# A linear-attention block with a gated convolution: the convolution moved to VectorE, g moved into x, the first loads split between two queues, and a new written-out order

## The chip, the cores and the metric

The kernel runs on one core of a Trainium2 chip. The metric is the device time of one execution in microseconds (us); less is better. The core's engines work from queues of their own, each strictly in its own order, and wait for each other on semaphores: TensorE (PE, matmuls into PSUM; its weight loads are shown apart as PEld), VectorE (DVE), ScalarE (ACT), GpSimd (POOL, which here only issues transfers) and SyncE (SP, which only issues transfers too).

## The reference

There are 8 batches (b), 8 heads, 576 rows (s), a head width of 64, a model width of 512 and a hidden width of 1024.

```
kv   = k^T v                          per batch and head, 64 x 64
o    = q kv
x    = o / sqrt(mean(o*o) + 1e-6) * g     (mean over the 64 of a head; heads side by side: 512)
h    = relu(x @ w_in)                 576 x 1024
c    = cw[0]*h[s-1] + cw[1]*h[s] + cw[2]*h[s+1]     per channel, zero outside
out  = (h * sigmoid(c)) @ w_out       576 x 512, fp32
```

All inputs and the output are fp32 in DRAM.

## The kernel before, in words

Everything on the chip is transposed: channels lie on the 128 partitions and the 576 rows of a batch along the free axis. The 512 model channels are 4 tiles t of two heads each; the 1024 hidden channels are 8 blocks f. The program is a list of small steps, written out by hand in the string ORDER (lines 62 to 105). A token such as `hm.3.4` calls the function `hm` with batch 3 and block 4, which issues its few instructions. The order of the tokens is the order of every engine's queue; the loop at line 540 ties each instruction to the one before it on its engine, so nothing is moved by a scheduler. The steps are:

- `Lq`, `Lk`, `Lv` (line 148): POOL loads q, k or v of a batch, cast from fp32 to bf16 on the way, into one of two buffers each. A buffer is free again when `qt` or `kv` of the batch that used it is done, and POOL waits for that with all that stands behind it.
- `kv` (272): k^T v on TensorE, 48 small matmuls; `kvc` (284, 286) copies it to a block-diagonal bf16 tile, on ScalarE, for batch 0 half on VectorE.
- `qt` (296): q transposed on TensorE, two tiles t in one step; `qc` (303) copies it to SBUF on VectorE. The rows stand in a permuted order (six interleaved groups of 96), which a later step undoes by a strided read (`natural`).
- `ot` (308, 309): o = q kv. `sq` (328) squares it and `oc` (334) copies it out, both on ScalarE.
- The norm: batch 0 by `on` (sums by a matmul with ones), `nl` (348, reciprocal square root on ScalarE) and `mu0` (357, x on VectorE). The others by `ss` (373), `ln` (383, with a table load before it and another before the next sigmoid), `sl` (391 to 394, the factor split in three bf16 parts), `sp` (403, spread back over the partitions by a matmul) and `mu` (409, x = o times the factor, on VectorE). Batch 1 has its own `ln`, then pairs 2 and 3, 4 and 5, 6 and 7.
- `ws` (261): g is multiplied into w_in on VectorE, from an fp32 staging tile to bf16. The staging tile comes in three pieces, one by SyncE and two by POOL.
- `hm` (426): one block f of x @ w_in, 8 matmuls of 288 columns; `re` (432): ReLU to bf16 on ScalarE.
- The convolution, in six groups c: batch 0; batch 1; batches 2 and 3; 4 and 5; 6; 7. For batch 0 it is done on TensorE: `di` (480) makes 24 diagonal matrices of cw on VectorE, `cv` (492) is six matmuls per block, `sv` (500) the sigmoid on ScalarE, `mv` (506) the product with h on VectorE. For the other groups: `ta` (451) makes three tap products of a block f on VectorE, `ad` (458, 459) adds them with a shift of one row, two blocks at a time, `sg` (465) takes the sigmoid of both blocks on ScalarE, `mg` (471) multiplies h by it on VectorE.
- `om` (516): 128 rows of the output, 8 matmuls of 512 columns, for a pair of batches p and one of nine row tiles m; `ea` (522) copies it out on ScalarE; `st` (532) stores it, on SyncE's queue.

PSUM is held in two pools: three large buffers ("a", for qt, ot, on, sp, hm, cv) and two small ones ("b", for kv, ss, om). Buffers of a pool are handed out in turn.

```python
CONV = {0: (0, 1, 'P'), 1: (1, 1, 'D'), 2: (2, 2, 'D'), 3: (4, 2, 'D'), 4: (6, 1, 'D'), 5: (7, 1, 'D')}
```

Each entry is (first batch, batches, engine).

## Time and profile before

| | |
|---|---|
| time, median of 3 runs | 203.81 us (203.37 to 204.84) |
| profiled execution: its span, first to last instruction | 201.0 us; the page gives no other time for it |
| busy: TensorE, VectorE, ScalarE | 175.3, 155.3, 145.9 us |
| granted TensorE clock | 1.000 |
| DMA: packets, bytes | 26295, 27.03 MB |
| transfers: median time from issue to landing | k, v, q pieces of 576 KB: 11.3, 13.6, 12.6 us; of 144 KB: 9.4 and 9.2 us; SyncE's 512 KB of w_in 3.4 us |
| VectorE: tap products; the two adds; product with h | 43.8; 19.8 + 20.1; 19.8 us |
| TensorE: hm, om (busy, matmuls overlap) | 69.9, 64.1 us |

The profile is one execution. Its page gives busy times, the span in 40 equal slices (each digit the busy tenths of 5 us), the chain of work that ended last, and groups of equal instructions with the mean duration of one. Sizes of transfers are those of the destination: a bf16 piece of 576 KB is 1.18 MB of fp32 in DRAM. A matmul's duration in the groups overlaps with its neighbours; its step from start to start is shorter.

### The profile page before, as it was taken

Reading aid. Unit: us, or ns where it says so; the run is one execution under the profiler, and the core shown is the slowest. Engines: PE = TensorE matmul, PEld = TensorE weight load, DVE = VectorE, ACT = ScalarE, POOL = GpSimd, SP = SyncE. Lnnn points to the kernel's source line nnn. Section 1 sums busy time; section 2 is a strip of 40 time slices with the busy share of each in tenths; the row PEclk is TensorE's granted clock in tenths of the full one; section 3 lists DMA queues with packets and bytes.
Section 4 is the critical chain, followed back from the end, with each engine's and each line's share of the span. In section 5 each row is a group of like instructions: output and inputs, shape, how many; then the busy total and the mean of one; then the engine's idle time right before and its main releaser. Section 6 shows DMA issues by size and latency. Waiting matters only on the chain.

```text
span 201.0 us, 4350 instructions
## 1 busy us (share of the span) xinstructions
PE 175.3 (87%) x1783; PEld 111.8 (56%) x1801; DVE 155.3 (77%) x325; ACT 145.9 (73%) x222; POOL 25.4 (13%) x38
## 2 busy tenths in 40 slices
PE   0057299799998999999999999999999999999792
PEld 0043057477775657766575776445667774444340
DVE  3097921458879799799899999989799999999400
ACT  2006516995999979999678899999978865684532
POOL 7373403103132303100000000000000000000000
PEclk9999999999999999999999999999999999999999
DMA  5999999999999999970200020070005001423654
GB/s 120 146 221 306 198 205 205 204 203 204 204 190 185 201 203 207 202 119 3 104 5 3 0 104 3 7 306 2 3 0 209 3 0 51 159 108 118 247 229 188
DMA packets 26295, 27.03 MB, mean 134 GB/s; under 512 B 1292, under 2 KB 21284, under 8 KB 26276
## 3 DMA queue, kind: packets, MB, share of 16 engines
q0 software_dynamic: 20368, 16.78, 52.4%
q1 hardware_dynamic: 5908, 9.98, 13.1%
q8 instruction: 14, 0.23, 0.4%
q14 instruction: 5, 0.04, 0.1%
HBM read 32.52 MB, written 9.44 MB: 209 GB/s over the span
## 4 chain that ended last, share of the span: by engine, by line
PE 59%; DVE 22%; DMA 10%; ACT 5%; issue 2%; POOL 1%; DVEq 0%; POOLq 0%; ACTq 0%
PE h_ps L426 25%; PE om_ps L516 18%; DVE tap L451 8%; DMA w_stage<-in_moe_w_in_dram 5%; DMA q_sb<-in_q_dram 5%; DVE h L471 4%; PE qt_ps L296 4%; DVE tap L459 3%; PE kv_ps L272 3%; PE sp_ps L403 3%; DVE tap L458 3%; PE cv_ps L492 3%; DVE xT L409 2%; PE o_ps L309 2%; ACT tap L465 2%
## 5 line engine op out<-in xcount | busy, mean ns | idle before, releaser
L426 PE MATMUL h_ps<-xT,w_in_sb 128*128 128x288 bf16 x512 | 69.9, 291 | 3.1 <-DVE w_in_sb L261 2.4
L516 PE MATMUL om_ps<-w_out_sb,h 128*128 128x512 bf16 x278 | 64.1, 379 | 1.5 <-DVE h L471 1.0
L426 PEld LDWEIGHTS <-w_in_sb 128*128 128x128 bf16 x512 | 49.9, 99 | 18.8 <-DVE w_in_sb L261 2.5
L432 ACT ACTIVATE h<-h_ps 128x576 bf16<-128x576 f32 x64 | 41.0, 656 | 14.9 <-PE h_ps L426 14.5
L516 PEld LDWEIGHTS <-h 128*128 128x128 bf16 x288 | 28.0, 98 | 32.2 <-DVE h L471 1.5
L451 DVE TENSOR_SCALAR tap<-h,cw 128x576 bf16<-128x576 bf16 (+1 forms) x120 | 43.8, 428 | 1.8 <-ACT h L432 1.3
L522 ACT ACTIVATE row<-om_ps 128x512 f32<-128x512 f32 x36 | 22.1, 618 | 15.6 <-PE om_ps L516 13.1
L465 ACT ACTIVATE tap<-tap 128x1152 bf16<-128x1152 bf16 (+1 forms) x20 | 31.1, 1553 | 1.6 <-DVE tap L459 1.5
L409 DVE TENSOR_TENSOR xT<-o,sp_ps 128x576 bf16<-128x576 f32 x28 | 20.1, 749 | 5.0 <-PE sp_ps L403 4.8
L471 DVE TENSOR_TENSOR h<-h,tap 128x1152 bf16<-128x1152 bf16 (+1 forms) x20 | 19.8, 992 | 1.8 <-ACT tap L465 1.8
L459 DVE TENSOR_TENSOR tap<-tap 128x1150 bf16<-128x1150 bf16 (+1 forms) x20 | 20.1, 1004 | 0.7
L303 DVE COPY qT<-qt_ps 128x1152 bf16<-128x1152 bf16 x16 | 11.8, 754 | 11.1 <-PE qt_ps L296 10.9
L458 DVE TENSOR_TENSOR tap<-tap 128x1150 bf16<-128x1150 bf16 (+1 forms) x20 | 19.8, 991 | 0.0
L328 ACT ACTIVATE sq<-o_ps 128x576 bf16<-128x576 f32 x28 | 18.2, 689 | 0.5 <-PE o_ps L309 0.5
L334 ACT ACTIVATE o<-o_ps 128x576 f32<-128x576 f32 x28 | 18.1, 677 | 0.5 <-ACT row L522 0.5
L286 ACT ACTIVATE kvbd<-kv_ps 64x256 bf16<-64x256 f32 (+1 forms) x18 | 6.0, 339 | 12.2 <-PE kv_ps L272 11.8
L148 POOL DMA_DIRECT2D k_sb<-in_k_dram x11 | 8.0, 723 | 35.9 <-PE kv_ps L272 35.9
L296 PE MATMUL qt_ps<-ident,q_sb 96*64 96x96 bf16 x384 | 11.2, 217 | 1.4 <-DMA q_sb<-in_q_dram 1.1
L296 PEld LDWEIGHTS <-q_sb 96*64 96x64 bf16 x384 | 9.6, 117 | 3.3 <-issue 2.1
L403 PE MATMUL sp_ps<-wparts,spread 128*128 128x288 bf16 x56 | 9.8, 286 | 0.2 <-DVE xT L409 0.2
L272 PEld LDWEIGHTS <-k_sb 96*64 96x64 bf16 x384 | 8.0, 123 | 3.3 <-issue 3.3
L309 PE MATMUL o_ps<-qT,kvbd 128*128 128x512 bf16 x25 | 9.6, 407 | 0.0
(55 smaller groups left out, 114.9 us busy)
## 6 DMA issues: line engine op xcount, KB each, us to landing
out_dram<-row SPq DMA_DIRECT2D x36, 256.0 KB, 2.3
q_sb<-in_q_dram POOLq DMA_DIRECT2D x8, 576.0 KB, 12.6
k_sb<-in_k_dram POOLq DMA_DIRECT2D x7, 576.0 KB, 11.3
v_sb<-in_v_dram POOLq DMA_DIRECT2D x7, 576.0 KB, 13.6
w_stage<-in_moe_w_in_dram POOLq DMA_DIRECT2D x1, 1024.0 KB, 9.9
w_out_sb<-in_moe_w_out_dram POOLq DMA_DIRECT2D x1, 1024.0 KB, 19.9
...
```

The source lines that it names most:

```text
L296: nc.tensor.transpose(ps[i * D:(i + 1) * D, tt, r * PS:(r + 1) * PS], q_sb[:, 2 * (2 * u + tt) + i, r * D:(r + 1) * D], ident[:PS, :PS])
L328: nc.scalar.activation(s.rearrange("p (n r) -> p n r", r=R), natural(src), AX.Square)
L409: nc.vector.tensor_mul(x_tile(b)[:, t, :].rearrange("p (e n) -> p e n", e=2), T["o32", b, t].rearrange("p (e n) -> p e n", e=2), T["sp", b ...
L426: nc.tensor.matmul(ps[:, e, :HS], w_in_sb[:, t, f * P:(f + 1) * P], x[:, t, e * HS:(e + 1) * HS], start=(t == 0), stop=(t == NT - 1))
L432: nc.scalar.activation(h_tile(b // 2)[:, f, b % 2, :].rearrange("p (e n) -> p e n", e=2), T["hm", b, f][:, :, :HS], AX.Relu)
L451: nc.vector.tensor_scalar_mul(tap[:, m, f % 2, :, :].rearrange("p b s -> p (b s)"), h_tile(p)[:, f, bs, :].rearrange("p b s -> p (b s)"), ...
L458: nc.vector.tensor_add(tap[:, 1, :, 1:], tap[:, 1, :, 1:], tap[:, 0, :, :S - 1])
L459: nc.vector.tensor_add(tap[:, 1, :, :S - 1], tap[:, 1, :, :S - 1], tap[:, 2, :, 1:])
L465: nc.scalar.activation(tap, tap, AX.Sigmoid)
L471: nc.vector.tensor_mul(h, h, T["tap", c, j][:, 1])
L516: nc.tensor.matmul(ps, h[:, f, m * P:(m + 1) * P], w_out_sb[:, f, :], start=(f == 0), stop=(f == NF - 1))
L522: nc.scalar.activation(T["os", p, m], T["om", p, m], AX.Copy)
```

## The change

- The convolution of batch 0 goes to VectorE like the others; `di`, `cv`, `sv`, `mv` and the diagonals are gone.
- The centre tap is no longer a product of its own. cw[0] and cw[2] are divided by cw[1] once (`pc`; cw[1] is kept away from zero), so c = cw[1] * (h + a*h[s-1] + b*h[s+1]), and cw[1] is the scale of the sigmoid's instruction. The scale is per block, so `sg` is one instruction per block f, not per two. `ta` makes two products, `aa` adds them with their shifts, `ab` adds h. The taps lie in two fixed tiles, rows 584 apart.
- g is multiplied into x: `mu` and `mu0` become scalar_tensor_tensor (o * g * factor). `ws` and the staging of w_in are gone; w_in is loaded straight to bf16 by POOL in two halves (`Li`), w_out in two halves (`Lo`).
- Batch 0: the heads of tiles t = 0, 1 come as fp32 by SyncE into the later h buffer and are cast by `ca` (q on ScalarE, k and v on VectorE); those of t = 2, 3 by POOL as before. `qt0` transposes one tile; `qc0` copies it on ScalarE and undoes the permutation there, so `mu0` reads plain rows. All `kvc` of batch 0 are on VectorE.
- Batch 1's loads are in halves of four heads. cw and g are issued from ScalarE's queue.
- `om` of the first and last pair of batches is in two steps of four blocks, with the same matmuls.
- Every buffer is named in the order (`hm.0.1@2`: PSUM buffer a2). The sets of buffers are as large as before. The order is new: among others batch 5's kv stands before batch 4's, and loads follow that.

```diff
-CONV = {0: (0, 1, 'P'), 1: (1, 1, 'D'), 2: (2, 2, 'D'), 3: (4, 2, 'D'), 4: (6, 1, 'D'), 5: (7, 1, 'D')}
+CONV = {0: (0, 1), 1: (1, 1), 2: (2, 2), 3: (4, 2), 4: (6, 1), 5: (7, 1)}
...
+pre@0,0,0,1 ca.q.0 qt0.0@0 qc0.0@0 ca.k.0 ca.v.0 kv.0.0.1@0 kvc.0.0.1.0 kvc.0.0.1.1 ot.0.0@1 sq.0.0@0 on.0@2
+ca.v.1 ca.k.1 ca.q.1 qt0.1@0 kv.0.1.1@1 kvc.0.1.1.1 nl.0@0 Lk.1.0@1 qc0.1 kvc.0.1.1.0 qt0.2@2 ot.0.1@0
+kv.0.2.1@0 qc0.2@1 sq.0.1@1 kv.0.3.1@1 on.1@2 kvc.0.2.1.0 mu0.0@0 kvc.0.2.1.1 nl.1@1 ot.0.2@1 kvc.0.3.1.0
+Lv.1.0@1 sq.0.2@2 ct@0 on.2@2 nl.2@2 kvc.0.3.1.1 mu0.1 Lq.1.0@1 Li.0 pc Lk.1.2 qt0.3@0 mu0.2 qc0.3 ot.0.3@2
+sq.0.3@3 kv.1.0.2@1 on.3@0 kvc.1.0.2.0 pl Lq.1.2 qt.1.0@1 nl.3@3 mu0.3 hm.0.0@0 re.0.0@0 qc.1.0@2 kvc.1.0.2.1
...
+    def ring(r, shape, dtype, name, **kw):
+        s = slots.pop(0)
+        p = psum if r in "ab" else work
+        return p.tile(shape, dtype, name=name, tag=f"{r}{s}", bufs=1, **kw)
...
+    def pre():
...
+        T["stg"] = ring("h", [PS, 3, 2, 2, R * D], FP32, name="stg")
+        for t in range(2):
+            for x in "kvq":
+                nc.sync.dma_start(out=T["stg"][:, "kvq".index(x), t], in_=heads(x, 0, 2 * t, 2))
+        nc.scalar.dma_start(out=cw_rows, in_=moe_conv_w.rearrange("k (f p) -> (k f) p", p=P))
+        for i in range(2):
+            nc.scalar.dma_start(out=g_sb[i * D:(i + 1) * D, :], in_=g_norm.unsqueeze(1))
+        act_table("rs")
...
+        for t in range(2, NT):
+            for x in "kvq":
+                nc.gpsimd.dma_start(out=qkv[x, 0][:, 2 * t:2 * t + 2, :], in_=heads(x, 0, 2 * t, 2))
...
+    def pc():
+        c1 = slice(NF, 2 * NF)
+        tmp = consts.tile([P, 3, NF], FP32, name="ctmp")
+        nc.vector.tensor_copy(cw, T["cw"])
+        nc.vector.tensor_scalar(tmp[:, 0], cw[:, c1], 0.0, 0.5, op0=AL.is_ge, op1=AL.subtract)
+        nc.vector.tensor_mul(tmp[:, 1], cw[:, c1], tmp[:, 0])
+        nc.vector.tensor_scalar(tmp[:, 1], tmp[:, 1], 5e-21, 4.0, op0=AL.max, op1=AL.mult)
+        nc.vector.tensor_mul(cw[:, c1], tmp[:, 0], tmp[:, 1])
+        nc.vector.reciprocal(tmp[:, 2], cw[:, c1])
+        nc.vector.tensor_mul(cw[:, 0:NF], cw[:, 0:NF], tmp[:, 2])
+        nc.vector.tensor_mul(cw[:, 2 * NF:], cw[:, 2 * NF:], tmp[:, 2])
...
+    def ca(x, t):
+        to, fr = qkv[x, 0][:, 2 * t:2 * t + 2, :], T["stg"][:, "kvq".index(x), t]
+        if x == "q":
+            nc.scalar.activation(to, fr, AX.Copy)
+        else:
+            nc.vector.tensor_copy(to, fr)
...
-        if b == 0 and i == 1:
+        if b == 0:
             nc.vector.tensor_copy(to, fr)
         else:
             nc.scalar.activation(to, fr, AX.Copy)
...
+    def qc0(t):
...
+        nc.scalar.activation(by_r(T["qT", 0, t]), natural(T["qt0", t][:, :S]), AX.Copy)
...
-        nc.vector.tensor_mul(
+        nc.vector.scalar_tensor_tensor(
             x_tile(b)[:, t, :].rearrange("p (e n) -> p e n", e=2),
-            T["o32", b, t].rearrange("p (e n) -> p e n", e=2), T["sp", b, t][:, :, :HS])
+            T["o32", b, t].rearrange("p (e n) -> p e n", e=2), g_sb[:, 0:1], T["sp", b, t][:, :, :HS],
+            op0=AL.mult, op1=AL.mult)
...
     def ta(c, f):
...
-        for m in range(3):
-            col = m * NF + f
-            nc.vector.tensor_scalar_mul(
-                tap[:, m, f % 2, :, :].rearrange("p b s -> p (b s)"),
-                h_tile(p)[:, f, bs, :].rearrange("p b s -> p (b s)"), cw[:, col:col + 1])
+        nc.vector.tensor_scalar_mul(tap[:, 0, f % 2, :n, 8:8 + S], h[:, f], cw[:, f:f + 1])
+        nc.vector.tensor_scalar_mul(tap[:, 1, f % 2, :n, :S], h[:, f], cw[:, 2 * NF + f:2 * NF + f + 1])
...
-        nc.vector.tensor_add(tap[:, 1, :, 1:], tap[:, 1, :, 1:], tap[:, 0, :, :S - 1])
-        nc.vector.tensor_add(tap[:, 1, :, :S - 1], tap[:, 1, :, :S - 1], tap[:, 2, :, 1:])
...
+    def aa(c, j):
+        n = CONV[c][1]
         tap = T["tap", c, j]
+        nc.vector.tensor_add(tap[:, 1, :, :n, :S], tap[:, 0, :, :n, 7:7 + S], tap[:, 1, :, :n, 1:1 + S])
...
+    def ab(c, j):
+        h, n = span(c)
+        y = T["tap", c, j][:, 1, :, :n, :S]
+        nc.vector.tensor_add(y, y, h[:, 2 * j:2 * j + 2])
...
-        tap = T["tap", c, j].rearrange("p m f b s -> p m (f b s)")[:, 1, :]
-        nc.scalar.activation(tap, tap, AX.Sigmoid)
+        y = T["tap", c, f // 2][:, 1, f % 2, :CONV[c][1], :S]
+        nc.scalar.activation(y, y, AX.Sigmoid, scale=cw[:, NF + f:NF + f + 1])
...
-        for f in range(NF):
-            nc.tensor.matmul(ps, h[:, f, m * P:(m + 1) * P], w_out_sb[:, f, :],
+        for f in range(f0, f0 + 4 if p in (0, 3) else NF):
+            nc.tensor.matmul(T["om", p, m], h[:, f, m * P:(m + 1) * P], w_out_sb[:, f, :],
                              start=(f == 0), stop=(f == NF - 1))
```

In the excerpt of the order, `pc`, `pl`, `ps`, `pn` and `ct` are the steps that make small constants; they stood ahead of the order before.

## The prediction

> **What bounds the kernel now.** I read the page's busy shares and slices first, to see which engine is full and when; then the busy times in four stretches cut at points of the order; then the chain of work that ended last; then the groups with their shapes, for prices; last the DMA rate of the first 40 us.
>
> ```profile
> PE 175.3 (87%) x1783; PEld 111.8 (56%) x1801; DVE 155.3 (77%) x325; ACT 145.9 (73%) x222; POOL 25.4 (13%) x38
> ...
> PE   0057299799998999999999999999999999999792
> ...
> DVE  3097921458879799799899999989799999999400
> ACT  2006516995999979999678899999978865684532
> ...
> DMA  5999999999999999970200020070005001423654
> ```
>
> The reader is to see a start of five slices (25 us) in which TensorE is mostly idle, then TensorE full to the end, with VectorE and ScalarE hardly less full beside it. The DMA engines are full for the first 17 slices, some 85 us.
>
> ```profile
> 0.00:25.53 25.53, 8.36 (x111) 5.08 (x114) 15.60 (x73) 7.37 (x13) 13.82 (x23) 1.00 1.05 198
> 25.53:75.65 50.12, 47.01 (x657) 32.51 (x664) 32.79 (x70) 40.16 (x68) 9.33 (x12) 1.00 1.30 200
> 75.65:188.69 113.04, 111.12 (x980) 70.38 (x990) 106.93 (x184) 95.22 (x137) 2.30 (x3) 1.00 0.30 82
> 188.69:201.00 12.31, 8.81 (x40) 3.84 (x40) 0.00 (x0) 3.11 (x6) 0.00 (x0) 1.00 0.55 213
> ```
>
> Columns: stretch, length, then busy time of PE, weight loads, DVE, ACT, POOL, granted clock, DMA share, GB/s. 25.53 is the first product with w_in (hm.0.0), 75.65 is kv.5, 188.69 the start of the last five output tiles. The clock is 1.00 throughout. From 75.65 to 188.69 TensorE (111.1 of 113.0) and VectorE (106.9) are both nearly full; shortening VectorE alone would soon meet TensorE.
>
> ```profile
> 1.29 9.51 DMA q_sb<-in_q_dram
> ...
> 12.59 9.87 DMA w_stage<-in_moe_w_in_dram
> 22.48 1.29 DVE w_in_sb L261
> ...
> 25.53 4.02 PE h_ps L426 x16
> ...
> 111.11 6.86 PE h_ps L426 x56
> ...
> 188.69 8.82 PE om_ps L516 x40
> ...
> 197.54 0.60 ACT row L522
> ```
>
> The chain (start, length, what) says why the start is long: the first q transfer, then the w_in staging, then its scaling by g. It also gives TensorE's true step prices, which the means of the groups overstate because matmuls overlap: 6.86/56 = 0.1225 for an h_ps matmul (0.98 per hm), 8.82/40 = 0.22 for om (1.73 for eight in the inner pieces). The same view gives kv 0.88, qt 0.65, ot and on 0.25, ss 0.30, sp 0.245, cv 0.74.
>
> ```profile
> L451 DVE TENSOR_SCALAR tap<-h,cw 128x576 bf16<-128x576 bf16 x72 | 22.2, 371 | 0.3 <-ACT h L432 0.2
> ...
> L465 ACT ACTIVATE tap<-tap 128x1152 bf16<-128x1152 bf16 x12 | 14.0, 1163 | 0.9 <-DVE tap L459 0.8
> ...
> L471 DVE TENSOR_TENSOR h<-h,tap 128x2304 bf16<-128x2304 bf16 x8 | 10.8, 1352 | 0.6 <-ACT tap L465 0.6
> L458 DVE TENSOR_TENSOR tap<-tap 128x2300 bf16<-128x2300 bf16 x8 | 10.8, 1352 | 0.0
> ...
> L392 DVE SCALAR_TENSOR_TENSOR rs<-hi,na,rs 128x288 f32<-128x288 bf16 x4 | 2.1, 518 | 0.1
> ```
>
> These are the shapes that the change reuses. L458 reads and writes from odd elements, L471 from even ones: the price is the same.
>
> **The change part by part, in step prices.** A step price is start to start behind a neighbour, as the timeline shows it: some 0.08 under the group's mean.
>
> *TensorE.* 64 hm x 0.98 + 36 om x 1.73 + 16 qt x 0.65 + 8 kv x 0.88 + 36 ot and on x 0.25 + 7 ss x 0.30 + 28 sp x 0.245 + 8 cv x 0.74 come to 166.3 before. The change drops the 48 cv matmuls (-5.9); batch 0's transposes go in four steps of 0.35 for two of 0.65 (+0.1): 160.5. Splitting om in halves costs nothing: the matmuls are the same 288.
>
> *VectorE.* A tap product costs 0.285 (576 elements) or 0.43 (1152). Per channel block two are left of three, and batch 0 comes in: 72 x 0.285 + 48 x 0.43 = 41.1 becomes 64 x 0.285 + 32 x 0.43 = 32.0. The adds stay two per pair; batch 0's convolution brings 4 aa, 4 ab, 4 mg (12 x 0.71 = 8.5) for 24 diagonals (4.5) and 8 products (3.4). The w_in scaling (2.8) goes, the four mu0 fall from 1.13 to 0.82 since both operands are now in one order, four k, v casts (0.6 each, from L261's 742 ns for 1024 fp32) come. Total 151.8 before, 142.5 after. The set-up steps (pc, pl, ps, pn: small ones of 0.06 to 0.2 and 1.23 for spread, as before) now stand among batch 0's mu0 and first taps; the w_in transfer covers pc and pl, ScalarE's longer work the others, and uncovered they cost some 4.
>
> *The product with g in mu* has no row at its size. The bf16 products leave 0.152 per instruction (752 ns at 1152, 1352 at 2304), so mu's 749 ns at 576 fp32 is 1.04 per element; L392 is 518 at 288, and 288 more elements give 0.82: +0.07 each, 28 times. Lower end 0; upper end 518 doubled, 1.04, +0.29 each (2.2 more in the VectorE stage below). I take +0.07, by the row of the same instruction.
>
> *aa* reads two tiles at odd elements; the row with one odd operand is L458. Lower end 0.68 and 1.28 (L458's steps), upper end the fp32 rate of mu, 0.6 and 1.2 more. By the upper VectorE has 37.6 in kv.5 to kv.6 (3 x 1.2 + 2 x 0.6 more) against TensorE's 34.1, and 5 x 1.2 more in kv.6 to hm.6.0, both stages of the sum below: 3.5 + 6.0 = 9.5 later. I take the lower, the nearer row. *ta* for two batches writes rows 584 apart instead of adjoining: lower end 0.43, upper end half rate, 0.3 more, 6 in the VectorE stage; taken 0.43.
>
> The Trainium skill, "VectorE: DVE Perf Modes", section "Mode 2×_1P — pack two bf16 into one 32-bit read", asks for 4-byte alignment, which speaks against aa; by it aa would run at its upper end in every conv, and the sum below would rise by about 9.6. L458 against L471 contradicts it, and the measurement decides.
>
> *ScalarE.* The sigmoid has a scale per channel block, so 20 + 8 become 48 instructions. From 2138 ns at 2304 and 1163 at 1152, one has 0.19 fixed: 20 more cost 3.8, less what overlap hides. Four qT copies (0.58) and two q casts (0.8) come, batch 0's four kvbd copies (0.35) go to VectorE. Total 143.5 before, 148.8 after; the eight table loads stay.
>
> *The queues.* SyncE no longer brings 0.5 MB of w_in but six fp32 pieces of two heads (295 KB each, 1.77 MB). POOL issues six such pieces, then k, v, q of batch 1 for four heads, then half of w_in straight to bf16. As before, its ninth transfer waits until the first has landed (4.2 us of POOL in the waits). cw and g go to ScalarE's queue, ahead of its table load: three issues at up to 0.6 each (SP's rows) and 1.28, done by 4, when nothing for ScalarE has landed. ca.q.1 stands ahead of nl.0 on ScalarE and waits for SyncE's sixth piece; that holds batch 0's first tile only, and its fourth is the last.
>
> ```profile
> GB/s 0 29 323 182 69 68 111 146 197 201 200 198 200 204 299 249 328 377 355 220 223 165 200 204 202 204 204 203 205 210 204 210 207 203 205 202 214 197 203 204
> ```
>
> One figure per us: between 4 and 8 us POOL's stream ran at 69 to 146 against 200 later, a hole of 0.4 MB in bf16, or 2 us. SyncE's pieces fill it: its 512 KB landed 3.4 us after the issue, POOL's first 9.5. By the Trainium skill, "DMA: Bandwidth & Descriptors", section "Issuing engines are not separate DMA queues", a second issuer saves only issue time; by it the 2 us would not come. The sum by it ends at 195.4, the second rival's price.
>
> *Start, to hm.0.0.* The tenth POOL transfer, half of w_in, stands behind 6.36 MB of source. Before, 5.64 MB had landed at 22.46 and 6.82 at 25.1 (issue of k for batch 1, 13.34 + 11.8): 24.0 between them. Less 2 to 3 for the hole: 21.3. The other path is q's last pair, 3.54 MB: 2.1 MB ahead of 22.46 at 0.44 per us (5.64 to 9.18 MB, 22.46 to 30.5) is 17.7, less 2 to 3 is 15; then qt0, qc0, ot, sq, on, nl, mu0 (0.35 + 0.66 + 0.6 + 0.65 + 0.8 + 0.74 + 0.82, with a kv and a qt step of 1.1 between), 20.7. So 21.3 for 25.5; bounds 18.3 (the transfers 3 earlier still) and 25.5.
>
> *hm.0.0 to kv.5.* TensorE has 33.6 there, VectorE 31.8, ScalarE 38.8: 15 re x 0.57, 24 sq and oc x 0.55, 11 sg x 0.59, 7 kvbd x 0.35, 2 ln with two table loads 3.0 each, 4 ea x 0.53. 21.3 + 38.8 = 60.1. The loads agree: k of batch 5 is last of 21.9 MB, which had landed at 63.4 before (q of batch 4), less 2 to 3: 60.4 to 61.4, or less with its gaps gone. Taken 60.0 (before: 75.65, with 7.9 more TensorE work in front).
>
> *kv.5 to the last om.* kv.5 to kv.6: TensorE 34.1, ACT 33.3, DVE 32.8. kv.6 to hm.6.0: DVE 42.8 (10 mu x 0.74, 5 aa x 1.28, 5 ab and 7 mg x 1.31, 20 ta x 0.43, 4 qc x 0.75, sl 1.65), TensorE 41.1. Rest: TensorE 46.3. Sum of the largest, 123.2. Before, the same stretch had 119.5 of TensorE work in 197.5 - 75.65 = 121.85, a factor of 1.02; 123.2 x 1.02 = 125.7. End 185.7. The last ea and store keep 3.5 (197.5 to 201.0). Behind hm.6.0 VectorE has 27.6 of work against 46.3, so the wait for the last mg (0.97 at 188.69 before) goes; TensorE's own work is next.
>
> Span 60.0 + 125.7 + 3.5 = 189.2, against 201.0. The page gives no other time for that execution; its span lies 2.8 under the median 203.8. I add 2.8: **192.0**.
>
> **The rivals.**
> *ScalarE becomes the bound* (0.15). Without overlap, by the group means, its 38.8 is 44.9: kv.5 at 66.2, time 198.2. For it: ACT shows slices of 9 from 40 to 65 us. Against: sq and oc start 0.53 to 0.55 apart there.
> *The transfers do not come earlier* (0.10): SyncE's pieces merely delay POOL's. Then kv.5 waits until 63.4: 195.4; with hm.0.0 at 25.5 too, 25.5 + 38.8 = 64.3 and 196.3. For it: DMA full until 85 us.
> *The loads of batches 4 and 6 come late* (0.05), the slower side. POOL's load of k for batch 6 waits for kv.5, and v of batch 4 stands behind it on POOL: issued at 61.5, wanted by kv.4 at 71. v of batch 6 is behind k and q of 7, which wait for kv.4 and qt.4.1: issued at 80.5, wanted at 94.8. At the landings of that time before (9.0 to 13.8) the stall is 0 to 4; at the longest, 23.0, it is 13.5 and again 8.7, time 214. It is slower than before from 11.8 us of stall in all.
>
> **How the numbers follow.** Forecast 0.62, with its own range 187 to 196; the first two rivals 0.25; the third 0.05; better than 187 (start at its lower bound, factor nearer 1) 0.05; within 1% of before (aa at its upper end in all stages: 201.6) 0.03. The upper bound takes in ScalarE's 198.2; the range is 187 to 198.5. A change under 1% is about what a measurement cannot tell from none. Faster by over 1% 0.92, within 1% 0.03, slower 0.05.
>
> **What would show it.** hm.0.0 near 21 and kv.5 near 60; ta 64 + 32 at 0.37 and 0.51; aa at the price of mg; mu near 0.82; no cv. It is wrong if TensorE waits for a load after kv.5, if ACT has no gaps past 75 us, or if aa costs twice mg.

## The result, and the profile after

| | before | after |
|---|---|---|
| time, median | 204.06 us (203.37 to 204.84, 4 runs) | 194.55 us (194.04 to 196.17, 4 runs) |
| ratio to before | | 0.9564, 95% interval [0.9512, 0.9615] |
| profiled execution: span | 201.0 us | 192.5 us (its time 194.67: 2.2 lie outside the span) |
| hm.0.0, kv.5, last om done | 25.53, 75.65, 197.51 us | 25.97, 65.45, 188.78 us |

The kernel is 4.4% faster. 192.0 was predicted, with a range of 187 to 198.5. The page of the kernel after, its busy shares and three of its rows of slices (one digit is 4.8 us):

```profile
PE 171.1 (89%) x1753; PEld 106.9 (56%) x1753; DVE 148.8 (77%) x279; ACT 153.5 (80%) x246; POOL 25.7 (13%) x39
...
PE   0047799899999999999999999999999999999992
...
DVE  3133839897988999999989999999989895977100
ACT  2047648999999899999999999999996869478431
```

TensorE's row starts as it did before: two empty slices, and full only from the sixth. What the change was to bring at the start did not come. The same execution in stretches, cut at hm.0.0, kv.5, kv.6, hm.6.0 and the end of the last om; the columns are the stretch, its length, the busy time of PE, weight loads, DVE, ACT and POOL, the granted clock, the DMA share and GB/s (the 1.00 ahead of 28.77 us stands for no record of the clock, see the last section):

```profile
0.00:25.90 25.90, 11.04 (x162) 6.51 (x162) 9.74 (x45) 11.19 (x16) 12.47 (x22) 1.00 1.06 197
25.90:65.45 39.55, 37.29 (x486) 24.08 (x486) 34.02 (x71) 35.60 (x62) 7.65 (x10) 1.00 1.29 203
65.45:100.58 35.13, 34.77 (x400) 23.45 (x402) 33.89 (x53) 34.60 (x58) 5.61 (x7) 1.00 0.94 156
100.58:142.50 41.92, 41.78 (x451) 26.90 (x451) 40.09 (x54) 40.66 (x61) 0.00 (x0) 1.00 0.13 48
142.50:188.78 46.28, 46.24 (x268) 25.97 (x266) 31.06 (x61) 30.80 (x52) 0.00 (x0) 1.00 0.34 125
```

Behind kv.5 TensorE is busy for 122.8 of the 123.3 us to the end of the last om: next to nothing makes it wait any more. From hm.0.0 to the last om there were 172.0 us before, with 166.9 of TensorE's busy time in them (the three later stretches shown of before), and there are 162.9 after, with 160.1. So of the 9.1 us gained there, 6.9 are matmuls that no longer stand there and 2.2 are waits that are gone. Of the 6.9, some 5.9 are the convolution's (eight blocks at 0.74); about 1 is not saved but moved: half of batch 1's kv and of its qt (24 matmuls each) now run ahead of hm.0.0. The start lost 0.4, the tail 0.2. That makes 8.5, the difference of the spans.

The chain of the kernel after (start, length, what) shows what the start waits for now:

```profile
3.41 11.13 DMA stg<-in_q_dram
14.54 0.02 issue
14.57 0.85 ACT q_sb L305
15.42 0.04 issue
15.46 0.69 PE qt_ps L343 x11
...
24.86 1.10 PE qt_ps L343 x24
25.97 1.07 PE h_ps L471 x4
```

Before, the staging of w_in and its scaling were the last thing ahead of hm.0.0. Now it is the sixth and last piece that SyncE brings, q of tile 1. It lands 11.13 us after its issue. ScalarE casts it at 14.57, and from there to hm.0.0 lie 11.4 us of steps of the tiles 1, 2 and 3, one after the other, and at their end 1.10 us of batch 1's transposition. The first half of w_in landed at 22.8 and was not waited for.

The groups of VectorE and ScalarE that the change made or reshaped (count, busy us, mean ns of one, idle time ahead):

```profile
L512 ACT ACTIVATE taps<-taps,cw 128x576 bf16<-128x576 bf16 x32 | 23.5, 775 | 1.0 <-DVE taps L506 0.9
L460 DVE SCALAR_TENSOR_TENSOR xT<-o,g_sb,sp_ps 128x576 bf16<-128x576 f32 x28 | 21.2, 810 | 1.8 <-PE sp_ps L454 1.8
...
L500 DVE TENSOR_TENSOR taps<-taps 128x2304 bf16<-128x2304 bf16 x8 | 10.9, 1358 | 0.1
L506 DVE TENSOR_TENSOR taps<-taps,h 128x2304 bf16<-128x2304 bf16 x8 | 10.8, 1355 | 0.2
L518 DVE TENSOR_TENSOR h<-h,taps 128x2304 bf16<-128x2304 bf16 x8 | 10.7, 1352 | 0.2 <-ACT taps L512 0.2
L494 DVE TENSOR_SCALAR taps<-h,cw 128x1152 bf16<-128x1152 bf16 x16 | 8.7, 544 | 0.0
```

### The profile page after: what moved, and what is told of

It reads as the page before. It is cut to its first block, busy times and chain, and to the rows that moved or that the text cites. A ratio compares the mean times of both kernels' runs of the same rounds, so it can differ in the third digit from the quotient of the medians.

```text
span 192.5 us, 4249 instructions
## 1 busy us (share of the span) xinstructions
PE 171.1 (89%) x1753; PEld 106.9 (56%) x1753; DVE 148.8 (77%) x279; ACT 153.5 (80%) x246; POOL 25.7 (13%) x39
## 4 chain that ended last, share of the span: by engine, by line
PE 70%; DVE 11%; ACT 8%; DMA 6%; issue 2%; SPq 1%; ACTq 0%
PE h_ps L471 28%; PE om_ps L528 27%; DMA stg<-in_q_dram 6%; PE qt_ps L343 4%; PE sp_ps L454 4%; PE kv_ps L319 3%; ACT sq L388 2%; PE o_ps L374 2%; DVE taps L493 2%; DVE taps L500 2%; DVE taps L506 2%; DVE taps L494 1%; ACT o L393 1%; ACT h L479 1%; DVE h L518 1%
## 5 line engine op out<-in xcount | busy, mean ns | idle before, releaser
L528 PE MATMUL om_ps<-w_out_sb,h 128*128 128x512 bf16 x288 | 66.7, 379 | 0.1
L512 ACT ACTIVATE taps<-taps,cw 128x576 bf16<-128x576 bf16 (+1 forms) x48 | 42.9, 933 | 1.0 <-DVE taps L506 0.9
L518 DVE TENSOR_TENSOR h<-h,taps 128x1152 bf16<-128x1152 bf16 (+1 forms) x24 | 22.7, 953 | 5.7 <-ACT taps L512 5.7
L500 DVE TENSOR_TENSOR taps<-taps 128x1152 bf16<-128x1152 bf16 (+1 forms) x24 | 23.0, 958 | 0.5
L343 PE MATMUL qt_ps<-ident,q_sb 96*64 96x96 bf16 x384 | 12.6, 221 | 12.0 <-ACT q_sb L305 11.9
L506 DVE TENSOR_TENSOR taps<-taps,h 128x1152 bf16<-128x1152 bf16 (+1 forms) x24 | 22.9, 956 | 0.5
L493 DVE TENSOR_SCALAR taps<-h,cw 128x576 bf16<-128x576 bf16 (+1 forms) x48 | 20.8, 434 | 2.5 <-ACT h L479 2.5
L460 DVE SCALAR_TENSOR_TENSOR xT<-o,g_sb,sp_ps 128x576 bf16<-128x576 f32 x28 | 21.2, 810 | 1.8 <-PE sp_ps L454 1.8
L494 DVE TENSOR_SCALAR taps<-h,cw 128x576 bf16<-128x576 bf16 (+1 forms) x48 | 20.3, 423 | 0.0
L374 PE MATMUL o_ps<-qT,kvbd 128*128 128x512 bf16 x32 | 12.7, 409 | 0.0
L276 POOL DMA_DIRECT2D q_sb<-in_q_dram x8 | 6.0, 748 | 34.5 <-PE qt_ps L343 29.0
```

The source lines that it names most:

```text
L343: nc.tensor.transpose(ps[i * D:(i + 1) * D, r * PS:(r + 1) * PS], qkv["q", b][:, 2 * t + i, r * D:(r + 1) * D], ident[:PS, :PS])
L493: nc.vector.tensor_scalar_mul(tap[:, 0, f % 2, :n, 8:8 + S], h[:, f], cw[:, f:f + 1])
L494: nc.vector.tensor_scalar_mul(tap[:, 1, f % 2, :n, :S], h[:, f], cw[:, 2 * NF + f:2 * NF + f + 1])
L500: nc.vector.tensor_add(tap[:, 1, :, :n, :S], tap[:, 0, :, :n, 7:7 + S], tap[:, 1, :, :n, 1:1 + S])
L506: nc.vector.tensor_add(y, y, h[:, 2 * j:2 * j + 2])
L512: nc.scalar.activation(y, y, AX.Sigmoid, scale=cw[:, NF + f:NF + f + 1])
```

## The experiments

The kernels named s1 to s7 and e1 to e3 start from the kernel after; the others say what they start from. "Theory A" is the prediction's: in each stretch the engine with the most work sets the time, ScalarE from hm.0.0 to kv.5, TensorE and VectorE nearly tied in the middle, TensorE at the end. The rivals are B (TensorE is the bound everywhere), C (VectorE is, to the end), and for the start D (SyncE's pieces share the DMA engines with POOL's and bring nothing), E (they win 2 us) and F (the transfers as a whole are the bound).

| kernel | time, median | ratio to before, 95% interval | hm.0.0 | kv.5 | kv.6 |
|---|---|---|---|---|---|
| after | 194.55 | 0.9564 [0.9512, 0.9615] | 25.97 | 65.45 | 100.58 |
| e1_pe_early | 199.28 | 0.9779 [0.9712, 0.9846] | 25.92 | 69.99 | 105.76 |
| e2_pe_late | 200.75 | 0.9868 [0.9804, 0.9933] | 27.24 | 66.51 | 101.75 |
| e3_third_tap | 202.91 | 0.9950 [0.9896, 1.0004] | 26.98 | 67.69 | 105.56 |
| b_centre_two_tiles (from before) | 204.63 | 1.0063 [1.0024, 1.0101] | 26.52 | 76.25 | |
| s1_pool_start | 192.49 | 0.9473 [0.9427, 0.9519] | 22.21 | 61.46 | 99.99 |
| s2_start_order | 193.26 | 0.9501 [0.9466, 0.9536] | 24.89 | 64.41 | 99.68 |
| s3_kvc_vector | 197.32 | 0.9700 [0.9643, 0.9756] | 26.01 | 67.90 | 102.97 |
| s4_no_g | 194.75 | 0.9568 [0.9524, 0.9613] | 26.02 | 65.24 | 100.54 |
| s5_v4_ahead (from s1) | 191.13 | 0.9403 [0.9361, 0.9444] | 22.23 | 62.00 | 97.06 |
| s6_tile_order (from s5) | 193.72 | 0.9542 [0.9497, 0.9587] | 20.15 | 65.64 | 100.69 |
| s7_setup_early (from s6) | 191.70 | 0.9431 [0.9366, 0.9495] | 20.00 | 62.24 | 97.28 |

The last three columns are of one profiled execution each. e1 and e2 leave everything ahead of hm.0.0 as it is in the kernel after (25.97), and theirs is at 25.92 and 27.24: one execution's start can lie 1.3 us off.

### More TensorE work, early and late

Eight times, 8 matmuls of 216 columns are put behind a step hm, of batch 1 (e1) or of batch 7 (e2). They write a part of the PSUM buffer that nobody reads. The chain of e2 prices them at 0.74 us for eight, 5.9 in all, the size of the convolution matmuls that the change took out.

```diff
+        if b == 1:          # e2: b == 7
+            for t in range(NT):
+                for e in range(2):
+                    nc.tensor.matmul(
+                        ps[:, e, HS:HS + 216], w_in_sb[:, t, f * P:(f + 1) * P], x[:, t, e * HS:e * HS + 216],
+                        start=(t == 0), stop=(t == NT - 1))
```

> The changed kernel with 8 matmuls of 216 columns added to each hm of batch 1 (64 in all, 8 x 8 x 0.09 = 5.8 us of TensorE work on PSUM columns that nobody reads; the output is the same). Seven of the eight blocks lie between hm.0.0 and kv.5. Theory A (between hm.0.0 and kv.5 ScalarE is the bound, 38.8 of work against TensorE's 33.6): most of it is covered, 1 to 3 us more. Theory B (TensorE is the bound everywhere behind hm.0.0): 5 to 6 us more. Theory C (VectorE is the bound to the end, as the chain of the kernel before showed): nothing.

> The same 64 added matmuls in the hm of batch 7, all behind hm.6.0, where TensorE has 46.3 of work against 27.6 of VectorE and 28.6 of ScalarE. Theories A and B: the whole 5.8 us more, 200.3. Theory C: under 2 us more.

Measured: e1 +4.7, e2 +6.2 us. In e1 kv.5 comes 4.5 us later than in the kernel after: the work that A held covered by ScalarE, up to kv.5, is mostly not covered. In e2 the stretch from kv.5 to the end of the span grows from 127.0 to 133.1, by 6.0 for 5.9 of work. In e2 both theories hold. In e1 the 4.7 lie 0.3 below B's 5 to 6 and well above A's 1 to 3, so B is the nearer. Seven of the eight added blocks, 5.2 us, stand ahead of kv.5 there, from 44.2 us on: all but 0.7 of it reaches kv.5. For the 18 us between hm.0.0 and the first of them e1 says nothing.

### The third tap back in, and the centre tap alone

e3 takes the centre tap out of the sigmoid's scale: VectorE makes three products again, and cw is not divided.

```diff
-    taps = [consts.tile([P, 2, 2, 2, TW], BF16, name=f"taps{i}") for i in range(2)]
+    taps = [consts.tile([P, 3, 2, 2, TW], BF16, name=f"taps{i}") for i in range(2)]
...
+        nc.vector.tensor_scalar_mul(tap[:, 2, f % 2, :n, :S], h[:, f], cw[:, NF + f:NF + f + 1])
...
-        nc.vector.tensor_add(y, y, h[:, 2 * j:2 * j + 2])
+        nc.vector.tensor_add(y, y, T["tap", c, j][:, 2, :, :n, :S])
...
-        nc.scalar.activation(y, y, AX.Sigmoid, scale=cw[:, NF + f:NF + f + 1])
+        nc.scalar.activation(y, y, AX.Sigmoid)
```

> The changed kernel with the centre tap as a third product on VectorE again (16 x 2 products of 576 and 16 of 1152 added, 32 x 0.285 + 16 x 0.43 = 16 us of VectorE work), ab adds that product, the sigmoid has no scale; order, instruction count of ScalarE and all else unchanged. Theory A, by the stage sums: 2.4 more between kv.5 and kv.6 and 4.3 more between kv.6 and hm.6.0, elsewhere covered: 6.7 more, 201. Theory B: 0 to 2 more. Theory C: 12 to 16 more.

Measured: +8.4 us, more than A's 6.7, and with it nearly the whole gain of the change is gone. The page of e3 gives VectorE 160.8 us of work for 148.8, and the chain by engine:

```profile
DVE 58%; PE 25%; DMA 6%; ACT 5%; issue 3%; SPq 1%
```

More than half of what ended last is now VectorE's. The two stretches from kv.5 to kv.6 and from there to hm.6.0, with VectorE's busy time as the third figure behind the length (the columns are those of the kernel after):

```profile
67.69:105.56 37.87, 34.88 (x396) 23.24 (x396) 36.84 (x62) 35.85 (x59) 5.38 (x7) 1.00 0.85 141
105.56:150.11 44.55, 42.05 (x451) 26.84 (x451) 43.56 (x64) 39.54 (x60) 0.00 (x0) 1.00 0.16 59
```

VectorE has become the bound: it is busy for 36.84 of 37.87 and 43.56 of 44.55 us. The two stretches are 2.7 and 2.6 us longer than in the kernel after, where A had 2.4 and 4.3. What goes beyond A's sum lies elsewhere in this execution: 1.0 ahead of hm.0.0, which is within what one start can be off, 1.2 from there to kv.5 and 0.4 behind hm.6.0.

The counterpart starts from the kernel before and makes the centre tap alone there, for batches 1 to 7; batch 0's convolution stays on TensorE.

```diff
+    def pc():            # the divided taps, as in the change
...
-        for m in range(3):
-            col = m * NF + f
-            nc.vector.tensor_scalar_mul(
...
+        nc.vector.tensor_scalar_mul(tap[:, 0, f % 2, :n, 8:8 + S], h[:, f], cr[:, f:f + 1])
+        nc.vector.tensor_scalar_mul(tap[:, 1, f % 2, :n, :S], h[:, f], cr[:, 2 * NF + f:2 * NF + f + 1])
...
-        nc.scalar.activation(tap, tap, AX.Sigmoid)
+        for f in (2 * j, 2 * j + 1):
+            y = T["tap", c, j][:, 1, f % 2, :n, :S]
+            nc.scalar.activation(y, y, AX.Sigmoid, scale=cr[:, NF + f:NF + f + 1])
```

> The kernel before with one part of the change alone: the centre tap in the sigmoid's scale for batches 1 to 7 (two tap products per channel block and two adds per pair, two fixed tap tiles that are handed out as they come free; a sigmoid with a scale per channel block). Batch 0's convolution stays on TensorE, and the loads, the order and the scaling by g stay. VectorE loses 24 products of 576 and 12 pairs of 1152 (some 10 us of work), ScalarE has 28 sigmoids more (about 5 us by their fixed part), TensorE's work stays at 161 us behind hm.0.0. Theory A (stage sums; TensorE and VectorE nearly tie from 75.65 us to hm.6.0): the stretch kv.6 to hm.6.0 loses the part in which VectorE was the longer, 2 to 3.5 us: 200.5 to 202. Theory B (TensorE bound everywhere): nothing, 203 to 204.5. Theory C (VectorE bound to the end): the whole 8 to 10 us, 194 to 196.

(A first version, e4_before_centre, handed its two tap tiles out strictly in turn, so that a group wrote into a tile whose content was still wanted. Its 209.15 us is the time of another computation and is not used.)

Measured: 204.63 for 203.56 of the kernel before on the same chip, 0.6% slower. B's 203 to 204.5 is missed by 0.1, A's 200.5 to 202 by more, C's by far. The stretch from kv.5, as it was cut for the kernel before (kv.5 at 76.25, the last five output tiles at 189.87):

```profile
76.25:189.87 113.62, 111.59 (x979) 70.36 (x991) 96.89 (x151) 99.40 (x155) 2.31 (x3) 1.00 0.29 79
```

The kernel before had 113.04 here, with PE 111.12 and DVE 106.93. VectorE does 10.0 us less, and the stretch is not a bit shorter, because TensorE fills it. The order was left as it was; one made for the shorter steps was not tried, but with TensorE busy for 111.6 of 113.6 us it could win about 2 there. In the same way e3 keeps the order of the kernel after. So the two parts belong together: all of the change without the centre tap gives 0.995 [0.9896, 1.0004], the centre tap alone 1.0063 [1.0024, 1.0101], and both 0.9564 [0.9512, 0.9615].

### The start: who brings the first heads

s1 takes SyncE's six fp32 pieces and their casts out; POOL brings all of batch 0, as bf16.

```diff
-        T["stg"] = ring("h", [PS, 3, 2, 2, R * D], FP32, name="stg")
-        for t in range(2):
-            for x in "kvq":
-                nc.sync.dma_start(out=T["stg"][:, "kvq".index(x), t], in_=heads(x, 0, 2 * t, 2))
...
-        for t in range(2, NT):
+        for t in range(NT):
...
+    def ca(x, t): pass
```

> The changed kernel with batch 0's first four heads loaded by POOL in bf16 like the others (pieces in the same order, no fp32 staging, no casts); all else as in the changed kernel. Theory D (SyncE's pieces share the DMA engines with POOL's and bring the start nothing; tile 1's q, which landed at 14.54, and the chain of small steps behind it set hm.0.0): hm.0.0 within 1.5 us of 25.9 and the time within 1.5 of 194.5. Theory E (the fp32 pieces do win the 2 us of the forecast, and only something behind them lost it): hm.0.0 and the time 2 to 4 later.

Measured: 192.49, 2.1 less, with hm.0.0 3.8 and kv.5 4.0 us earlier. SyncE's pieces, with their casts and with the place of those casts in the queues, were not only no gain, they were the loss. The DMA rate of the first 40 us, one figure per us, in bytes as they arrive, with the sums of the queues (packets, MB, share). First the kernel after:

```profile
GB/s 0 37 270 269 98 170 147 201 278 281 263 238 237 203 201 204 201 205 204 205 205 203 203 204 203 204 207 205 204 204 204 204 203 217 194 204 201 205 203 204
...
q0 software_dynamic: 7967, 6.16, 99.3%
q1 hardware_dynamic: 1248, 1.77, 14.8%
```

Then s1:

```profile
GB/s 0 12 4 108 86 96 175 188 188 191 192 201 198 199 205 200 201 204 207 217 193 202 204 201 204 207 207 200 210 202 206 202 204 202 204 206 200 205 203 203
...
q0 software_dynamic: 9260, 7.08, 117.2%
```

By its rate the kernel after is far ahead: its first 15 figures sum to 2.89 MB, those of s1 to 2.04. But a byte of SyncE's pieces is fp32, and one of POOL's is bf16, half as much of the source. In source bytes the kernel after has 1.77 + 2 x 1.12 = 4.0 MB after 15 us, when SyncE's last piece has landed, and s1 has 2 x 2.04 = 4.1. After 40 us they stand at 1.77 + 2 x 6.16 = 14.1 and 2 x 7.08 = 14.2. The hole was filled with bytes and with nothing else. What is worse, the pieces delay each other: q of tile 0 landed at 9.4 after and at 7.55 in s1, q of tile 1 at 14.54 against the 11.09 at which s1's qt0.1 runs; POOL's pieces of 144 KB took 9.1 to 10.2 us from issue to landing after, 5.2 to 5.5 in s1 (medians). That is what the Trainium skill's page "DMA: Bandwidth & Descriptors" says in "Issuing engines are not separate DMA queues": transfers of all issuing engines interleave on the same 16 DMA engines, and a second issuer saves issue time alone. E falls. D is right that the pieces bring nothing, but its 1.5 us were too narrow: they cost 3.8 at hm.0.0 and 2.1 in the time.

Of the 4 us only 2.1 reach the end. The chain of s1:

```profile
11.88 10.29 DMA w_in_sb<-in_moe_w_in_dram
22.21 2.04 PE h_ps L463 x8
...
61.46 0.88 PE kv_ps L311 x48
64.13 10.26 DMA v_sb<-in_v_dram
74.44 0.97 PE kv_ps L311 x48
```

Now w_in is what hm.0.0 waits for, and kv.4 at 74.44 waits for v of batch 4, issued at 64.13 behind POOL's wait for kv.5. This is the mechanism of the third rival. In the profiled execution the wait had a second price. The busy times and the granted clock (the third figure from the end) before and behind kv.4:

```profile
71.81:75.23 3.42, 1.63 (x55) 1.30 (x53) 3.42 (x7) 2.18 (x4) 0.58 (x1) 1.00 0.79 100
75.23:78.64 3.41, 3.41 (x23) 2.04 (x18) 3.33 (x4) 2.10 (x4) 0.77 (x1) 0.50 1.04 143
```

TensorE's clock was granted at half for 3.41 us, at most 1.7 us of its work: 40 matmuls of hm behind kv.4 take 6.25 us for 4.90 in the kernel after. This execution took 193.92 us, the other three 192.24 to 192.51. So the 99.99 of s1's kv.6 holds more than the wait itself. In the kernel after, kv.4 came at 76.64 and the chain does not pass through that load; in s4, with the same loads and order, it just does (issued 67.18, 9.38 us, kv.4 at 76.60). So there was next to no slack left: an earlier start has this load for its next deadline.

s5 removes it. POOL issues v of batch 4 ahead of k of batch 6:

```diff
-mu.3.2 Lk.4.0@1 re.2.0@1 kvc.5.0.4.0 mg.1.2 mu.3.3 Lk.6.0@0 ta.1.2@1 kvc.5.0.4.1 hm.2.5@1 re.2.5 sp.3.0@2
-Lv.4.0@1 mu.3.0 ta.1.3 aa.1.1 mg.1.3 hm.2.7@0 ab.1.1 re.2.7 ot.5.0@1 sq.5.0@0 ta.1.0@0 hm.2.1@2 oc.5.0@2 re.2.1
+mu.3.2 Lk.4.0@1 Lv.4.0@1 re.2.0@1 kvc.5.0.4.0 mg.1.2 mu.3.3 Lk.6.0@0 ta.1.2@1 kvc.5.0.4.1 hm.2.5@1 re.2.5 sp.3.0@2
+mu.3.0 ta.1.3 aa.1.1 mg.1.3 hm.2.7@0 ab.1.1 re.2.7 ot.5.0@1 sq.5.0@0 ta.1.0@0 hm.2.1@2 oc.5.0@2 re.2.1
```

> The kernel of s1_pool_start (all of batch 0's and 1's inputs by POOL, 192.49) with one load moved on POOL: v of batch 4 is issued ahead of k of batch 6, so that it no longer stands behind POOL's wait for kv.5. In s1 kv.4 waited for that transfer, 10.26 us long, and TensorE stood for about 1.8 us. Theory A (the queue position is the cause): v of batch 4 is issued some 4 us earlier, the wait at kv.4 goes, kv.6 comes 1.5 to 2 us earlier than 99.99, time 190.5 to 191. Theory F (the transfers as a whole are the bound there, and it is only the last of them that shows): the wait stays or another load takes its place, 192 to 192.8.

Measured: 191.13, 0.1 above A's 190.5 to 191 and well below F's 192, and the lowest median of all kernels here (s7's interval overlaps with it): 3.4 us below the kernel after, of the 3.7 by which its hm.0.0 is earlier. The stretches of s5 from hm.0.0, cut as in the kernel after:

```profile
22.23:62.00 39.77, 37.15 (x478) 24.16 (x486) 33.40 (x70) 35.54 (x62) 8.73 (x11) 1.00 1.30 204
62.00:97.06 35.06, 34.24 (x396) 23.37 (x402) 33.87 (x53) 34.53 (x58) 4.61 (x6) 1.00 1.02 173
97.06:139.30 42.24, 41.70 (x449) 27.15 (x454) 40.41 (x55) 40.95 (x61) 0.00 (x0) 1.00 0.14 51
```

kv.6 comes 2.9 us earlier than in s1's profile, of which up to 1.7 are the half clock there. 39.77, 35.06 and 42.24 stand against 39.55, 35.13 and 41.92. Behind hm.0.0 it is the same kernel, moved.

### The start: the order of the tile steps

s2 leaves the transfers of the kernel after and puts tile 2, which POOL brings, ahead of tile 1, whose q comes late. With it nl.0 goes ahead of the cast that waits for tile 1, pc and pl go behind mu0.3, and qt0 uses the smaller PSUM buffers.

```diff
...
-ca.v.1 ca.k.1 ca.q.1 qt0.1@0 kv.0.1.1@1 kvc.0.1.1.1 nl.0@0 Lk.1.0@1 qc0.1 kvc.0.1.1.0 qt0.2@2 ot.0.1@0
+ca.k.1 ca.v.1 qt0.2@0 kv.0.2.1@1 nl.0@0 kvc.0.2.1.1 kvc.0.2.1.0 mu0.0@0 Lk.1.0@1 qc0.2@1 ot.0.2@2 ca.q.1
+qt0.1@0 kv.0.1.1@1 kvc.0.1.1.0 kvc.0.1.1.1 sq.0.2@2 on.2@0 qc0.1 qt0.3@0 kv.0.3.1@1 ot.0.1@1 kvc.0.3.1.0 kvc.0.3.1.1
...
```

> The changed kernel with the steps ahead of hm.0.0 in another order and no other change of work: tile 2 (its q landed at 12.6) before tile 1 (14.54), nl.0 ahead of the cast that waits for tile 1, pc and pl behind mu0.3, and the transposes of batch 0 in the small PSUM buffers, so that tile 3 need not wait for mu0.1. Theory D (the data were there by 15.4 and w_in by 22.8; the order of the small steps makes hm.0.0 late): hm.0.0 at 22.8 to 24, the time 2 to 3 lower, 192. Theory F (the transfers bound the start and the stretch behind it): hm.0.0 earlier but kv.5 where it was, the time within 0.7.

Measured: 193.26, 1.3 less, with hm.0.0 1.1, kv.5 1.0 and kv.6 0.9 us earlier. That is less than D's 2 to 3 and more than F's 0.7, and F's kv.5, which was to stay, moves along. The order of the steps is thus worth something, and what is won at hm.0.0 arrives at the end; but 1.1 us at hm.0.0 is no more than one start can be off, the interval [0.9466, 0.9536] overlaps with that of the kernel after, and how much of it is the cast ca.q.1 was not separated from the other moves.

s6 goes further from s5: batch 0's tiles strictly in turn, the first half of w_in issued ahead of batch 1's loads, hm.0.0 to hm.0.2 between batch 1's first steps, and the set-up steps pc and pl behind hm.0.0.

```diff
...
-sq.0.3@3 kv.1.0.2@1 on.3@0 kvc.1.0.2.0 pl Lq.1.2 qt.1.0@1 nl.3@3 mu0.3 hm.0.0@0 re.0.0@0 qc.1.0@2 kvc.1.0.2.1
-hm.0.1@2 ot.1.0@1 re.0.1 Lv.1.2 qt.1.1@0 Li.1 ta.0.0@0 hm.0.2@2 ps ta.0.1 qc.1.1@3 sq.1.0@4 oc.1.0@4 re.0.2 pn
+sq.0.3@3 on.3@0 ct@0 Lq.1.2 nl.3@3 mu0.3 hm.0.0@0 re.0.0@0 kv.1.0.2@1 kvc.1.0.2.0 kvc.1.0.2.1 pc
+hm.0.1@2 re.0.1 qt.1.0@1 qc.1.0@2 Lv.1.2 Li.1 hm.0.2@0 ot.1.0@1 ta.0.0@0 re.0.2 pl qt.1.1@2 ps ta.0.1 qc.1.1@3 sq.1.0@4 oc.1.0@4 pn
...
```

> s5_v4_ahead with the first 35 us reordered as well: batch 0's tile steps in strict order of arrival, qt0 in the smaller PSUM buffers, the first half of w_in issued ahead of batch 1's loads, hm.0.0 to 0.2 between batch 1's first steps, and the set-up steps pc and pl behind hm.0.0. Same work, same bytes. Theory A (the wait for w_in and the steps around tile 3 set hm.0.0, and what is behind follows it one for one): hm.0.0 at 19.5 to 20.5 for 22.2 in s1, kv.5 earlier by 1.5 to 2.5, time 188 to 189.5. Theory F (batch 1's loads, which now land about 2.6 us later, take it back at kv.1 and qt.1): hm.0.0 earlier, kv.5 the same as in s5_v4_ahead within 0.5, time 190.3 to 191.3.

Measured: hm.0.0 at 20.15 as wished, and the time 193.72, worse than s5 by 2.6 and worse than both expectations. The chain of s6 behind hm.0.2, and what stands in it:

```profile
25.04 1.12 PE qt_ps L335 x24
...
28.91 1.23 DVE spread L257
30.14 0.47 DVE taps L485
30.61 0.27 DVE taps L486
30.89 0.68 DVE qT L360
31.56 0.04 issue
31.60 1.14 PE h_ps L463 x8
```

In s5 batch 1's first q copy ran at 22.1, ahead of the taps and of spread; in s6 its loads came later, it ran at 26.2, and the set-up steps (masks, then spread) fell between the two q copies. ot.1.1 waited for the second of them, and hm.0.3 stood behind ot.1.1 in TensorE's queue. And the wait had a second price here too. The busy times and the granted clock (the third figure from the end) of s6, in short stretches:

```profile
28.00:30.00 2.00, 0.67 (x31) 0.59 (x27) 1.72 (x8) 1.92 (x5) 1.22 (x1) 1.00 1.31 205
30.00:32.00 2.00, 0.40 (x4) 0.32 (x4) 1.95 (x8) 0.68 (x2) 2.00 (x3) 1.00 1.31 208
32.00:34.00 2.00, 2.00 (x14) 1.10 (x12) 1.95 (x5) 1.22 (x3) 1.53 (x3) 0.71 1.33 200
34.00:35.00 1.00, 1.00 (x6) 0.63 (x5) 0.97 (x4) 1.00 (x3) 0.00 (x0) 0.50 1.32 204
35.00:36.00 1.00, 1.00 (x11) 0.16 (x9) 0.73 (x1) 0.60 (x2) 0.00 (x0) 0.50 1.32 205
36.00:37.00 1.00, 1.00 (x11) 0.72 (x8) 0.25 (x1) 0.78 (x2) 0.00 (x0) 0.88 1.31 201
```

TensorE did 1.07 us of work in 4 us, and after that its clock was granted at half for 3.41 us, from 32.84 to 36.25. All four executions of s6 have a granted clock of 0.989 to 0.991 over their span, so this is in each of them: at most 1.7 us of the 2.6. The Trainium skill's page "TensorE: Matmul & The Clock Gate" has this in its Part 1 on the clock gate: after an idle window of about 3.4 us the clock falls to half, and it returns after as long a time of work. The rows agree in size, though TensorE was not quite idle here.

s7 moves the set-up steps (pl, ps, pn) to the place where VectorE waits for tile 1's loads, and hm.0.3 ahead of ot.1.1. The loads stay as in s6.

```diff
-qt0.1@0 kv.0.1.1@1 nl.0@0 kvc.0.1.1.0 kvc.0.1.1.1 mu0.0@0 qc0.1 ot.0.1@2 sq.0.1@1
+qt0.1@0 kv.0.1.1@1 nl.0@0 pl ps pn kvc.0.1.1.0 kvc.0.1.1.1 mu0.0@0 qc0.1 ot.0.1@2 sq.0.1@1
...
-hm.0.1@2 re.0.1 qt.1.0@1 qc.1.0@2 Lv.1.2 Li.1 hm.0.2@0 ot.1.0@1 ta.0.0@0 re.0.2 pl qt.1.1@2 ps ta.0.1 qc.1.1@3 sq.1.0@4 oc.1.0@4 pn
-kv.1.2.2@0 ta.0.2@1 kvc.1.2.2.0 ot.1.1@1 kvc.1.2.2.1 hm.0.3@2 sq.1.1@5 oc.1.1@5 re.0.3 ot.1.2@0 aa.0.0 sq.1.2@6
+hm.0.1@2 re.0.1 ta.0.0@0 qt.1.0@1 qc.1.0@2 Lv.1.2 Li.1 hm.0.2@0 ot.1.0@1 re.0.2 ta.0.1 qt.1.1@2 qc.1.1@3 sq.1.0@4 oc.1.0@4
+kv.1.2.2@0 ta.0.2@1 kvc.1.2.2.0 kvc.1.2.2.1 hm.0.3@2 re.0.3 ot.1.1@1 sq.1.1@5 oc.1.1@5 ot.1.2@0 aa.0.0 sq.1.2@6
```

> s6_tile_order with VectorE's set-up steps (pl, ps, pn: selection masks, spread, the constants of the square root, some 3.0 us) moved from between batch 1's two q copies to the third tile's wait for its loads, and hm.0.3 moved ahead of batch 1's second product with kvbd. Same loads in the same order as s6. In s6 hm.0.0 came at 20.15 as wished, but VectorE ran spread between 26.9 and 30.1, its second q copy at 30.8, and hm.0.3 waited for it until 31.60. Theory S (the place of the set-up steps took the gain back): hm.0.3 at 28 to 29.2, kv.5 earlier than s6's 65.64 by 2.4 to 3.6, time 190 to 191.3, about s5_v4_ahead's 191.13 or a little less. Theory L (batch 1's loads, which land some 2.6 us later than in s5, took it back): hm.0.3 earlier, but the next steps of batch 1 wait for k, v and q, kv.5 within 1 of 65.64, time 192.7 to 193.8.

Measured: hm.0.3 at 28.10, kv.5 3.4 us earlier than in s6, the time 191.70, 0.4 over S's 190 to 191.3. Theory L falls, and S holds but for these 0.4: the place of the small steps, and with it the clock, had taken the gain back. In s7 the clock is at 1.00 from 25 to 40 us. How much is the set-up steps' place and how much is hm.0.3, which was moved too, was not separated. But its head start of 2.2 us at hm.0.0 over s5 is gone all the same: the 16 matmuls behind batch 1's ss stand at 32.81 in s7 and at 32.63 in s5, and ScalarE is busy for 9.74 of the 10 us from 30 to 40. Whether ScalarE or the arrival of batch 1's loads levels the two was not separated.

### ScalarE as the bound from hm.0.0 to kv.5, and the product with g

s3 gives the copies kvbd of batches 1 to 3 to VectorE, for ScalarE, which by A was the bound there.

```diff
-        if b == 0:
+        if b <= 3:
             nc.vector.tensor_copy(to, fr)
```

> The changed kernel with the kvbd copies of batches 1, 2 and 3 on VectorE (7 of 0.35 and one more off ScalarE, about 2.5 us, in the stretch from hm.0.0 to kv.5). Theory A (ScalarE bounds that stretch, 38.8 against VectorE's 31.8 and TensorE's 33.6): 1.5 to 2.5 lower, 192.5. Theories B and F (TensorE or the transfers bound it): within 0.7.

Measured: +2.8 us instead of -2, with kv.5 at 67.90, 2.5 later. All three expectations miss. It does not clear ScalarE: the copies went to VectorE, which has 36.8 us of work in the longer stretch for 34.0, and the chain of s3 passes through VectorE's set-up steps, taps and copies from 28.76 to 34.18. What it shows is that there is no room for them in VectorE's queue.

s4 leaves g out (a product of two for the product of three in mu and mu0), so that only the instruction's form is priced.

```diff
...
-        nc.vector.scalar_tensor_tensor(
-            x_tile(0)[:, t, :], T["ot", 0, t][:, :S], g_sb[:, 0:1], T["rs0", t], op0=AL.mult, op1=AL.mult)
+        nc.vector.tensor_mul(x_tile(0)[:, t, :], T["ot", 0, t][:, :S], T["rs0", t])
...
```

> The changed kernel without g: mu and mu0 are plain products of two tensors; the product with g is left out. This measures what the scalar_tensor_tensor costs: about 0.06 each by the groups (810 against 749 ns), 28 and 4 of them. Theory A: only the ten mu between kv.6 and hm.6.0 count, if at all: 0 to 0.7 lower. Theory C: 2 lower.

Measured: 194.75 for 194.55, no difference. The instruction is 810 ns for the 750 of the product in s4, and none of it that the runs can tell reaches the end.

## Why the prediction was right, and where it was wrong

The profiled execution is 2.7 us over the 192.0. By the prediction's own steps: start +4.6, hm.0.0 to kv.5 +0.8, kv.5 to the last om -2.4, tail +0.2, outside the span -0.6. That the total is no further off is in part luck: a start that missed by 4.6 was half paid back by a factor that was not needed.

- **The step that failed is the start: "SyncE's pieces fill the hole", "less 2 to 3".** 21.3 was predicted for hm.0.0, 25.9 measured. w_in, whose landing gave the 21.3, came at 22.8; the other 3.1 are the tiles' steps, priced to end at 20.7. The hole was filled with fp32 bytes, at the price of POOL's pieces. Two premises fell: that SyncE's pieces would land as its 512 KB did before (3.4 us for the only large one; now 3.3 for the first of six and 11.1 for the last), and that ca.q.1 holds "batch 0's first tile only". It held tile 1, and with it everything that stood behind in the queues of ScalarE and TensorE. TensorE's transposition of one tile also cost 0.69 there for the 0.35 it was priced at (the last section has why). The second rival had the first of these, and its time with hm.0.0 at 25.5 was 196.3; its price of 195.4 came nearest to the 194.55. s1 and s5 show what the start is worth: with it at 22.2, and v of batch 4 moved, the time is 191.1.
- **hm.0.0 to kv.5: 38.8 predicted, 39.55 measured, but by a wrong reason.** ScalarE was priced at 38.8 and is busy for 35.6. TensorE was priced at 33.6 and is busy for 37.3: in this stretch eight matmuls of hm take 1.1 us and the first ones 2, for the 0.98 that was taken from a later, undisturbed place. e1 (5.2 us of matmuls ahead of kv.5, +4.5) shows that from 44 us on TensorE sets the time. Before that it is not settled: from 30 to 40 us ScalarE is busy for 9.5 of 10 and TensorE for 8.75, and s3 does not part them. The rival "ScalarE becomes the bound" had 44.9 of ScalarE's work; 35.6 were measured (and the slices of 9 that it names are broken by a 5 at 45 to 50 us).
- **kv.5 to the last om: 125.7 predicted, 123.3 measured.** Before the factor of 1.02 the sum was 123.2. The factor, which stood for waits, was not needed: TensorE is busy for 122.8. But two of its terms miss and cancel: kv.5 to kv.6 took 35.1 for 34.1, kv.6 to hm.6.0 41.9 for 42.8. In the latter VectorE was over-priced, 42.8 for 40.1, and TensorE's 41.8 is the longer, so the tie goes to TensorE. That TensorE would be next once VectorE is shorter was right, and stronger than put: on the kernel before, the centre tap alone gives nothing. "The clock is 1.00 throughout" was wrong for the first 30 us (last section).
- **The prices.** aa at 1358 ns costs as much as mg at 1352, so the upper end, half rate at odd elements, did not come, and the Trainium skill's alignment rule ("VectorE: DVE Perf Modes", "Mode 2×_1P") does not hold here. mu: 0.82 predicted, 0.81 measured. ta for two batches: 0.43 as a step, 533 and 544 ns as means, for some 0.51. The sigmoids: 775 and 1251 ns.
- **The third rival** did not show in the kernel after, but was near: v of batch 4 came with no slack (s4), and with the earlier start of s1 it did hold kv.4 up; s5 puts that right.
- **Better than predicted would have been possible.** With batch 0 brought by POOL alone and one load moved (s5), the time is 191.13, 0.9403 [0.9361, 0.9444] of the kernel before.
